# Attention with a step for row maxima: half of the weighted-value groups cut into two column halves, the output copied out by ScalarE alone, the maxima transposed one place later in VectorE's order

## The chip, the core and the metric

The kernel runs on one core of one Trainium2 chip. The metric is device time in microseconds for one execution; the time of a kernel is the median of several executions.

## What is computed

The reference is one transformer block without learned norms: layer norm, softmax attention with 32 heads of 16 columns, a residual, layer norm, a gMLP mixer, a residual. The change concerns the attention alone.

```
x: 1 x 2048 x 512;  H = 32 heads, Dh = 16
q, k, v = split(layernorm(x) @ wqkv)
p = softmax(q k^T * Dh**-0.5)          # 32 heads, 2048 x 2048 scores each
o = p v
h = x + o @ wo
z = gelu(layernorm(h) @ w_in);  z1, z2 = halves of z
out = h + (z1 * (w_sp @ layernorm(z2) + b_sp)) @ w_out
```

## The kernel before

**Stages.** First the projections q, k, v (about 0 to 165 us of the profile); then the attention (about 165 to 1410 us); then the output projection, the gMLP product with the 2048 x 2048 matrix `w_sp`, and the last projection.

**Units of the attention.** The heads are taken four at a time (8 groups `hg`), the queries 512 at a time (4 blocks `qb`), the keys 128 at a time (16 blocks `kb`). That makes 512 units. The loop takes two units in each turn, a *pair*: `kb` even, then `kb1` odd. Every 8 pairs one block of 512 queries is finished.

**Scores.** `score(hg, qb, kb, p)` (L673, L676) makes one tile `s` of 128 keys by 2 heads by 512 queries: two matmuls with 50 rows each, one on the rows from 0 and one on the rows from 64 of the array (`t` = 0 and 1), so that these two can run side by side. ScalarE then takes the exponential of the whole tile (1024 columns) into `pt`. A unit has two such tiles, a pair four. Below they are called S0 and S1 (first unit), S' and S'' (second unit). The pool `ps_s` has two places for `s`, which the four tiles use in turn: S0 and S' the one, S1 and S'' the other. So S' waits for the exponential of S0, and S'' for that of S1.

**Weighted values.** `weigh` (L684) adds one unit to the block's output `pv`: four matmuls, one for each head, each 32 columns of the array wide and 512 queries long, side by side. They are float32; the trace shows each as two matmuls, eight in a group. The groups run one unit late: in a pair, the group of the previous pair's second unit comes first (`prev`), and that of the pair's own first unit at the end. One column of the weights is of ones, so that `pv` also carries the softmax sums. `pv` has one PSUM bank.

**Maxima.** The exponent needs each query's largest score. `max_pair(m)` computes it ahead for 128 queries and two heads, in eight steps, each a matmul with 48 rows into one of three PSUM banks (`ps_m`, banks 0 to 2; L225): four steps on the rows from 64 (`four[0]` to `four[3]`, t = 1), two on the rows from 0 (`two` and the step for keys 1536 to 2047, t = 0), each followed by a maximum over 512 columns on VectorE (L230); and `minus` and `plus` (t = 0) for the other keys: ScalarE takes the absolute value of the differences (`minus`, L235), and VectorE adds that to the sums and reduces (`plus`, L239). The pairs of the loop make the maxima 11 pairs ahead: 245 pairs of the 256 hold these eight steps, the last 11 hold none. After every eighth `max_pair` VectorE reduces the parts (L245, `nm`), GpSimd splits them, and `max_rows` (L259, L263) transposes them on VectorE and issues eight DMAs on SyncE's queue that put them into two extra rows of `qst`.

**End of a query block.** At `kb` = 0, `gather` copies `pv` of the finished block to `o`: columns 0 to 255 by VectorE (L690), the others by ScalarE (L694), one after the other. Then eight DMAs store `o` and the sums. At `kb` = 6 `invert` (L648) takes the reciprocal of the sums on VectorE.

**Order.** Inside the attention the order of each engine's instructions is the order in which the code issues them (a manual schedule for TensorE, ScalarE, VectorE and SyncE). A pair before the change, in TensorE's order, where a step's number after "bank" is its PSUM bank:

```
S0, S1, four[0] (bank 2), two (bank 0), group of prev,
minus (bank 1), [gather at kb = 0], four[1] (2), S', four[2] (0), S'',
four[3] (1), plus (2), group of the first unit, [max_rows], last (1)
```

The code that the change touches:

Of the kernel before, what the change touches and what calls it, by code (L numbers as in the profile page):

```python
# [8 lines left out]
F32 = mybir.dt.float32  # L9
# [3 lines left out]
AF = mybir.ActivationFunctionType  # L13
# [5 lines left out]
P = 128  # L19
# [3 lines left out]
DH = 16  # L23
# [3 lines left out]
NB = S // P  # L27
HB = NB // 2
NQ = S // 512
DB = D // P  # L30
HG = H // 4
# [17 lines left out]
def block_kernel(ctx: ExitStack, tc: tile.TileContext, x, wqkv, wo, w_in, w_sp4, b_sp, w_out, out):  # L49
# [154 lines left out]
            return more[i]()  # L204
        return ps_m.tile([P, 512], F32, name=f"m{i}")

    def max_pair(m):

        g, i = divmod(m, 8)
        hg, qb = divmod(g, NQ)
        q, k, w = qst[g], kst[hg % 2], uvs[hg % 2]
        if i == 0:
            mx[g] = sm.tile([P, 16, 4], F32, name="mx")
            nc.gpsimd.memset(mx[g][:, :8, 3:], LOW)
        c, p = slice(i % 4 * P, i % 4 * P + P), i // 4
        at = lambda t, e: mx[g][:, t * 8 + i, e:e + 1]  # L220

        def scores(t, keys, b):
            r = slice(RG * t, RG * t + KS)
            acc = bank(b)
            nc.tensor.matmul(acc, q[r, p, c], keys[r, p], start=True, stop=True)  # L225
            return acc

        def one(t, e, b):
            acc = scores(t, k[:, :, 512 * e:512 * e + 512], b)
            nc.vector.reduce_max(at(t, e if t else e - 1), acc, axis=AX.X)  # L230

        def minus(b):
            acc = scores(0, w[:, :, 512:], b)
            ab[0] = sm.tile([P, 512], F32, name="ab")
            nc.scalar.activation(ab[0], acc, AF.Abs)  # L235

        def plus(b):
            acc = scores(0, w[:, :, :512], b)
            nc.vector.tensor_tensor_reduce(ab[0], acc, ab[0], 0.5, LOW, ALU.add, ALU.max, at(0, 0))  # L239

        def last(b):
            one(0, 3, b)
            if i == 7:
                nm = sm.tile([P, 2, 8], F32, name="nm")
                nc.vector.tensor_reduce(nm.rearrange("p t i -> p (t i)"), mx.pop(g), axis=AX.X,  # L245
                                        op=ALU.max, negate=True)
                parts = sm.tile([P, 2, 2, 8], F32R, name="mparts")
                split(parts[:, :, 0], parts[:, :, 1], nm, "pool", "pool")
                turned[0] = (g, parts)

        ab = {}
        four = [lambda b, e=e: one(1, e, b) for e in range(4)]
        return [four[0], lambda b: one(0, 2, b), minus, four[1], four[2], four[3], plus, last]

    def max_rows():

# [398 lines left out]
    with ExitStack() as at:  # L655
# [6 lines left out]
        ps_s = at.enter_context(tc.tile_pool(name="ps_s", bufs=2, space=PSUM))  # L662
        pv = {}

        def score(hg, qb, kb, p):

            q, k = qst[hg * NQ + qb], kst[hg % 2]
            turn[0] += len(later)
            pool = later[0] if later and turn[0] % 3 == 2 else ps_s
            s = pool.tile([P, 2, 512], F32, name="s")  # L670
            for t in range(2):
                r = slice(RG * t, RG * t + KM)
                nc.tensor.matmul(s[:, t, :], k[r, p, kb * P:(kb + 1) * P], q[r, p, :],  # L673
                                 start=True, stop=True)
            t = pp.tile([P, 2, 512], F32, name="pt")
            nc.scalar.activation(t, s, AF.Exp, scale=DH ** -0.5)  # L676
            return t

        def weigh(hg, qb, kb, pts):
            if kb == 0:  # L680
                pv[0] = ps_v.tile([P, 512], F32, name="pv")
            for j in range(4):
                c = (4 * kb + j) * VW
                nc.tensor.matmul(pv[0][32 * j:32 * j + 32, :], vst[hg % 2][:, c:c + 32],  # L684
                                 pts[j % 2][:, j // 2, :], start=kb == 0, stop=kb == NB - 1)

        def gather(hg, qb, pool=sm):

            o = pp.tile([P, 512], F32, name="o", bufs=1)
            nc.vector.tensor_copy(o[:, :256], pv[0][:, :256])  # L690
            if pool is sm and later:
                nc.vector.tensor_copy(o[:, 256:], pv[0][:, 256:])
            else:
                nc.scalar.activation(o[:, 256:], pv[0][:, 256:], AF.Copy)  # L694
            cols = slice(qb * 512, (qb + 1) * 512)
            sums = pool.tile([P, 16], F32, name="sums")
            for j in range(4):
                h = head(hg, j % 2, j // 2)
                nc.sync.dma_start(o_scr[h * DH:(h + 1) * DH, cols], o[32 * j:32 * j + DH, :])
                nc.sync.dma_start(sums[32 * j:32 * j + 32, :], o[32 * j + DH:32 * j + VW, :])  # L700
            sums_[0] = (hg, cols, sums, pool)
# [18 lines left out]
        def more_h(k):  # L720

            for _ in range(k):
                if not pieces:
                    sb = h_rows[len(hns)]
                    acc = later[0].tile([P, 512], F32, name="h")
                    pieces.extend([sb, acc, h_products(sb, acc)])
                sb, acc, products = pieces
                next(products)
                made[0] += 1
                if made[0] % (3 * DB):  # L730
                    continue
                pieces.clear()
                add_h(sb, acc)
                split_o(h_rows[len(hns) + 1], *("pool", "pool") if hns else [None])
                mv, rs = scale_h(sb)
                hns[sb] = e2.tile([P, D], F32, name="hn", bufs=3)
                nc.vector.tensor_scalar(hns[sb], xrs.pop(sb), mv[:, 0:1], rs,
                                        op0=ALU.subtract, op1=ALU.mult)
# [4 lines left out]
        with tc.manual_schedule(engines={E.PE, E.Activation, E.DVE, E.SP}):  # L743
            for n in range(0, len(units), 2):
                (hg, qb, kb), (_, _, kb1) = units[n:n + 2]
                if hg + 1 < HG and n % 64 < 24 and n % 4 == 0:
                    load_k(hg + 1, [n % 64 // 4])
                if hg + 1 < HG and n % 64 < 12 and n % 4 == 2:
                    load_uv(hg + 1, [n % 64 // 4])
                if hg + 1 < HG and n % 64 == 30:  # L750
                    load_v(hg + 1)
                if kb == 2 and n // NB + 3 < HG * NQ:
                    load_q(n // NB + 3)
                steps = max_pair(m) if m < 8 * HG * NQ else []
                m += 1
                if not steps and not later:
                    maxima.close()
                    later.append(attn.enter_context(
                        tc.tile_pool(name="ps_l", bufs=1, space=PSUM, side="right")))
                step = lambda b: steps and steps.pop(0)(b)  # L760
                pts = [score(hg, qb, kb, 0), score(hg, qb, kb, 1)]
                step(2)
                step(0)
                if prev is None:

                    pv[0] = ps_v.tile([P, 512], F32, name="pv")
                    for j in range(4):
                        nc.tensor.matmul(pv[0][32 * j:32 * j + 32, :], vst[0][:, :32],
                                         vst[0][:, :512], start=True, stop=True)
                else:  # L770
                    weigh(*prev)
                step(1)
                if kb == 0 and n:
                    gather(*units[n - 1][:2])
                step(2)
                pts1 = [score(hg, qb, kb1, 0)]
                step(0)
                pts1.append(score(hg, qb, kb1, 1))
                step(1)
                step(2)  # L780
                if n >= 490:
                    more_h(2 + (n < 494))
                weigh(hg, qb, kb, pts)
                if turned:
                    max_rows()
                step(1)
                prev = (hg, qb, kb1, pts1)
                if kb == 6 and n > NB:
                    invert()
                if n % 32 == 16 and n < 6 * 32:  # L790
                    load_weights(n // 32)
                if n in (476, 482, 492, 504):
                    load_o(h_rows[(476, 482, 492, 504).index(n)])
                if n == 482:
                    split_o(h_rows[0], "pool", "pool")
            weigh(*prev)
            gather(*prev[:2], e2)
# [186 lines left out]
    with ExitStack() as fin:  # L984
# [29 lines left out]
        def product(acc, a, b, blocks=range(HB)):  # L1014
            for k in blocks:
                mm3(acc, a[0][:, k, :], a[1][:, k, :], b[0][:, k, :], b[1][:, k, :],
                    k == 0, k == HB - 1)
# [299 lines left out]
```

## Time and profile before

| | |
|---|---|
| median of 3 runs | 1864.46 us (1864.09 to 1864.78) |
| the profiled execution | 1863.55 us |
| its span, first to last instruction | 1861.7 us |
| TensorE busy / VectorE / ScalarE / GpSimd | 1852.8 / 1530.4 / 1317.8 / 225.7 us |
| exponentials of the attention (L676) | 1024 instructions, 994.1 us |
| maxima on VectorE (L230, L239) | 1508 and 249 records, 956.6 and 169.6 us |
| weighted values on TensorE (L684) | 4096 matmul records, 545.8 us |
| granted TensorE clock | 1.000 |

The busy time of TensorE is modelled from pipelined matmuls, and a few records can be missing, so a busy share near 100% does not say that TensorE works at its peak: a matmul that waits behind another one counts as busy. What the other engines and the order in time say has to be read beside it. Groups of instructions give the busy time, the mean of one and what ended the idle time before them; a chain of waits follows the end of the program back from releaser to releaser.

### The profile page before, as it was taken

How to read it: one execution, taken by the hardware profiler on the slowest of the kernel's cores; microseconds unless marked ns; L12 is line 12 of the kernel's file. 1: busy time of each engine (PE TensorE's matmuls, PEld its weight loads, DVE VectorE, ACT ScalarE, POOL GpSimd, SP SyncE). 2: the span in 40 equal slices, each digit the busy share in tenths (PEclk: the TensorE clock that was granted, in tenths of full speed). 3: DMA queues.
4: the chain of work that ended last, by engine and by line, in shares of the span. 5: the costliest groups of instructions: out<-in, count | busy, mean ns of one | idle time of the engine just before them, and what ended most of it. 6: DMA issues, size and time to landing. Idle time of an engine off the chain costs nothing.

```text
span 1861.7 us, 31964 instructions
## 1 busy us (share of the span) xinstructions
PE 1852.8 (100%) x11410; PEld 1047.3 (56%) x11410; DVE 1530.4 (82%) x3060; ACT 1317.8 (71%) x1696; POOL 225.7 (12%) x305
## 2 busy tenths in 40 slices
PE   9999999999999999999999999999999999999999
PEld 6775444444444444444444444444437889999998
DVE  6487999999999999999999999999935766877664
ACT  3224888888888888888888888888895444434221
POOL 2241000011010100000000000000001756001111
PEclk9999999999999999999999999999999999999999
DMA  6688111221120121022011112100123555768662
GB/s 192 193 191 197 41 24 30 48 53 28 39 57 15 49 44 25 13 51 40 13 39 32 23 29 50 25 14 13 30 56 108 175 160 166 226 186 264 212 191 94
DMA packets 148743, 159.90 MB, mean 86 GB/s; under 512 B 63096, under 2 KB 93320, under 8 KB 147240
## 3 DMA queue, kind: packets, MB, share of 16 engines
q1 hardware_dynamic: 143800, 146.44, 29.7%
q10 hardware_dynamic: 4752, 11.41, 1.6%
q8 instruction: 90, 1.47, 0.3%
q14 instruction: 69, 0.57, 0.1%
q0 software_dynamic: 32, 0.01, 0.0%
HBM read 101.26 MB, written 55.61 MB: 84 GB/s over the span
## 4 chain that ended last, share of the span: by engine, by line
PE 98%; DVE 1%; issue 0%; ACT 0%; DMA 0%; SPq 0%; POOL 0%; POOLq 0%; DVEq 0%; ACTq 0%
PE pv L684 27%; PE m L225 26%; PE s L673 13%; PE acc L96 5%; PE acc L98 5%; PE acc L97 5%; PE g L98 4%; PE g L97 4%; PE g L96 4%; PE acc L617 2%; PE tp L1189 1%; PE h L617 0%; PE tp L885 0%; PE acc L1210 0%; PE tp L369 0%
## 5 line engine op out<-in xcount | busy, mean ns | idle before, releaser
L676 ACT ACTIVATE pt<-s 128x1024 f32<-128x1024 f32 x1024 | 994.1, 1030 | 141.6 <-PE s L673 139.2
L230 DVE TENSOR_REDUCE mx<-m 128x1 f32<-128x512 f32 x1508 | 956.6, 684 | 99.7 <-PE m L225 56.6
L225 PE MATMUL m<-kst,qst 48*128 48x512 f32 x1508 | 605.1, 447 | 0.0
L684 PE MATMUL pv<-pt,vst 128*32 128x512 f32 x4096 | 545.8, 605 | 0.0
L673 PE MATMUL s<-qst,kst 50*128 50x512 f32 x2048 | 465.1, 428 | 0.0
L225 PEld LDWEIGHTS m<-kst,qst 48*128 48x128 f32 x1508 | 262.7, 184 | 316.2 <-DVE mx L230 221.4
L673 PEld LDWEIGHTS s<-qst,kst 50*128 50x128 f32 x2048 | 222.6, 185 | 53.9 <-ACT pt L676 29.8
L225 PE MATMUL m<-uvs,qst 48*128 48x512 f32 x497 | 246.5, 496 | 0.0
L225 PEld LDWEIGHTS m<-uvs,qst 48*128 48x128 f32 x497 | 90.8, 183 | 205.4 <-DVE mx L230 204.6
L684 PEld LDWEIGHTS pv<-pt,vst 128*32 128x32 f32 x4096 | 80.8, 108 | 158.2 <-issue 155.5
L239 DVE CUSTOM_DVE_ANT_0 ab<-m,ab 128x512 f32<-128x512 f32 x249 | 169.6, 681 | 0.0
L235 ACT ACTIVATE ab<-m 128x512 f32<-128x512 f32 x248 | 149.3, 602 | 4.1 <-PE m L225 4.0
L90 POOL CAST mparts<-nm 128x16 fp32r<-128x16 f32 x32 | 6.3, 197 | 880.2 <-DVE nm L245 880.2
L825 ACT ACTIVATE ws<-a 128x512 fp32r<-128x512 f32 x80 | 45.8, 621 | 50.0 <-PE g L98 23.6
L904 ACT ACTIVATE z<-acc 128x464 f32<-128x464 f32 (+2 forms) x64 | 27.6, 456 | 65.3 <-PE acc L98 63.3
L96 PE MATMUL acc<-wi,hT 128*128 128x464 f32 (+2 forms) x196 | 72.8, 371 | 0.0
L98 PE MATMUL acc<-wi,hT 128*128 128x464 f32 (+2 forms) x196 | 71.8, 366 | 0.0
L97 PE MATMUL acc<-wi,hT 128*128 128x464 f32 (+2 forms) x196 | 71.6, 365 | 0.0
L826 DVE TENSOR_TENSOR ws<-a,ws 128x512 fp32r<-128x512 f32 x80 | 56.1, 745 | 13.1 <-ACT ws L825 13.0
L96 PE MATMUL g<-b,ws 128*128 128x344 f32 x192 | 62.6, 326 | 0.0
L88 ACT ACTIVATE part<-acc 128x512 fp32r<-128x512 f32 x32 | 19.1, 598 | 60.8 <-PE acc L98 56.0
L98 PE MATMUL g<-t,ws 128*128 128x344 f32 x192 | 61.3, 319 | 0.0
(200 smaller groups left out, 2121.2 us busy)
## 6 DMA issues: line engine op xcount, KB each, us to landing
a<-in_w_sp SPq DMA_DIRECT2D x80, 256.0 KB
qst<-q_scr SPq DMA_DIRECT2D x192, 64.0 KB
z_scr<-z ACTq DMA_DIRECT2D x32, 344.0 KB
kst<-k_scr SPq DMA_DIRECT2D x42, 256.0 KB
k_scr<-part SPq DMA_DIRECT2D x16, 512.0 KB
q_scr<-part SPq DMA_DIRECT2D x16, 512.0 KB
z<-z_scr SPq DMA_DIRECT2D x14, 344.0 KB
b<-z_scr SPq DMA_DIRECT2D x24, 172.0 KB
```

The costliest lines, as they stand in the source:

```text
L96: nc.tensor.matmul(ps, lh, rh, start=first, stop=False)
L97: nc.tensor.matmul(ps, lh, rl, start=False, stop=False)
L98: nc.tensor.matmul(ps, ll, rh, start=False, stop=last)
L225: nc.tensor.matmul(acc, q[r, p, c], keys[r, p], start=True, stop=True)
L230: nc.vector.reduce_max(at(t, e if t else e - 1), acc, axis=AX.X)
L235: nc.scalar.activation(ab[0], acc, AF.Abs)
L239: nc.vector.tensor_tensor_reduce(ab[0], acc, ab[0], 0.5, LOW, ALU.add, ALU.max, at(0, 0))
L673: nc.tensor.matmul(s[:, t, :], k[r, p, kb * P:(kb + 1) * P], q[r, p, :], start=True, stop=True)
L676: nc.scalar.activation(t, s, AF.Exp, scale=DH ** -0.5)
L684: nc.tensor.matmul(pv[0][32 * j:32 * j + 32, :], vst[hg % 2][:, c:c + 32], pts[j % 2][:, j // 2, :], start=kb == 0, stop=kb == NB - 1)
L825: nc.scalar.activation(hi, src, AF.Copy)
L826: (nc.gpsimd if el == "pool" else nc.vector).tensor_sub(lo, src, hi.bitcast(F32))
```

## The change

Only the 245 pairs with maxima change, and `gather`. The order of the eight steps of `max_pair` in the loop becomes `minus, four[0], two, (keys 1536 on), four[1], four[2], plus, four[3]`; elsewhere it stays. The score tiles S1 and S'' are made in two pieces, each of one matmul, with other work between the two (`scores_of`). The group of `prev` is cut into two halves of 256 columns each, set apart, in every pair but those with `kb` = 0 (214 pairs). `gather` copies all 512 columns of `pv` by ScalarE in 30 of its 32 calls. `max_rows` runs after the first VectorE step of the following pair and no longer at that pair's end. A pair after the change, in TensorE's order:

```
minus (bank 2), S0 (both), four[0] (1), [max_rows], S1 first piece,
half group of prev (at kb = 0 the whole, then gather),
two (0), S1 second piece, keys 1536 on (1), four[1] (2), S' (both),
other half group of prev (not at kb = 0),
S'' first piece, four[2] (0), plus (1), S'' second piece,
group of the first unit, four[3] (0)
```

The matmuls of the weighted values become 1192 of 512 columns and 1712 of 256 columns in the program, where there were 2048 of 512 columns. No other engine gets more or fewer instructions but VectorE and ScalarE for `gather`: 30 copies of 256 columns less on VectorE, and on ScalarE 30 of 512 columns in place of 30 of 256.

```diff
         ab = {}
         four = [lambda b, e=e: one(1, e, b) for e in range(4)]
-        return [four[0], lambda b: one(0, 2, b), minus, four[1], four[2], four[3], plus, last]
+        two = lambda b: one(0, 2, b)
+        if late:
+            return [minus, four[0], two, lambda b: one(0, 3, b), four[1], four[2], plus,
+                    lambda b: last(b, 1, 3)]
+        return [four[0], two, minus, four[1], four[2], four[3], plus, lambda b: last(b, 0, 3)]
...
-        def score(hg, qb, kb, p):
+        def score(*unit):
+            first, second = scores_of(*unit)
+            first()
+            return second()
+
+        def scores_of(hg, qb, kb, p):
...
-            for t in range(2):
+
+            def product(t):
                 r = slice(RG * t, RG * t + KM)
                 nc.tensor.matmul(s[:, t, :], k[r, p, kb * P:(kb + 1) * P], q[r, p, :],
                                  start=True, stop=True)
-            t = pp.tile([P, 2, 512], F32, name="pt")
-            nc.scalar.activation(t, s, AF.Exp, scale=DH ** -0.5)
-            return t
-
-        def weigh(hg, qb, kb, pts):
+            def second():
+                product(1)
+                t = pp.tile([P, 2, 512], F32, name="pt")
+                nc.scalar.activation(t, s, AF.Exp, scale=DH ** -0.5)
+                return t
+
+            return lambda: product(0), second
+
+        def weigh(hg, qb, kb, pts, cols=slice(0, 512)):
...
-                nc.tensor.matmul(pv[0][32 * j:32 * j + 32, :], vst[hg % 2][:, c:c + 32],
-                                 pts[j % 2][:, j // 2, :], start=kb == 0, stop=kb == NB - 1)
+                nc.tensor.matmul(pv[0][32 * j:32 * j + 32, cols], vst[hg % 2][:, c:c + 32],
+                                 pts[j % 2][:, j // 2, cols], start=kb == 0,
+                                 stop=kb == NB - 1 and cols.stop == 512)
 
         def gather(hg, qb, pool=sm):
             o = pp.tile([P, 512], F32, name="o", bufs=1)
-            nc.vector.tensor_copy(o[:, :256], pv[0][:, :256])
-            if pool is sm and later:
-                nc.vector.tensor_copy(o[:, 256:], pv[0][:, 256:])
+            if pool is sm and not later:
+                nc.scalar.activation(o, pv[0], AF.Copy)
             else:
-                nc.scalar.activation(o[:, 256:], pv[0][:, 256:], AF.Copy)
+                nc.vector.tensor_copy(o[:, :256], pv[0][:, :256])
...
-                step = lambda b: steps and steps.pop(0)(b)
-                pts = [score(hg, qb, kb, 0), score(hg, qb, kb, 1)]
-                step(2)
-                step(0)
...
+                if steps:
+                    step = lambda b: steps.pop(0)(b)
+                    step(2)
+                    pts = [score(hg, qb, kb, 0)]
+                    step(1)
+                    if turned:
+                        max_rows()
+                    first, second = scores_of(hg, qb, kb, 1)
+                    first()
...
+                        weigh(*prev, *[slice(0, 256)] * (kb > 0))
+                        if kb == 0:
+                            gather(*prev[:2])
+                    step(0)
+                    pts.append(second())
+                    step(1)
+                    step(2)
+                    pts1 = [score(hg, qb, kb1, 0)]
+                    if kb:
+                        weigh(*prev, slice(256, 512))
+                    first, second = scores_of(hg, qb, kb1, 1)
+                    first()
+                    step(0)
+                    step(1)
+                    pts1.append(second())
+                    weigh(hg, qb, kb, pts)
+                    step(0)
```

More of the change, by code (lines that the diff above doesn't have):

```diff
@@ L205, in bank, with max_pair @@
         return ps_m.tile([P, 512], F32, name=f"m{i}")
-    def max_pair(m):
+    def max_pair(m, late=False):
         g, i = divmod(m, 8)
@@ L239, in plus, with last @@
             nc.vector.tensor_tensor_reduce(ab[0], acc, ab[0], 0.5, LOW, ALU.add, ALU.max, at(0, 0))
-        def last(b):
-            one(0, 3, b)
+        def last(b, *which):
+            one(*which, b)
             if i == 7:
@@ L683, in weigh @@
                 c = (4 * kb + j) * VW
-                nc.tensor.matmul(pv[0][32 * j:32 * j + 32, :], vst[hg % 2][:, c:c + 32],
-                                 pts[j % 2][:, j // 2, :], start=kb == 0, stop=kb == NB - 1)
+                nc.tensor.matmul(pv[0][32 * j:32 * j + 32, cols], vst[hg % 2][:, c:c + 32],
+                                 pts[j % 2][:, j // 2, cols], start=kb == 0,
+                                 stop=kb == NB - 1 and cols.stop == 512)
         def gather(hg, qb, pool=sm):
             o = pp.tile([P, 512], F32, name="o", bufs=1)
-            nc.vector.tensor_copy(o[:, :256], pv[0][:, :256])
-            if pool is sm and later:
-                nc.vector.tensor_copy(o[:, 256:], pv[0][:, 256:])
-            else:
-                nc.scalar.activation(o[:, 256:], pv[0][:, 256:], AF.Copy)
+            if pool is sm and not later:
+                nc.scalar.activation(o, pv[0], AF.Copy)
+            else:
+                nc.vector.tensor_copy(o[:, :256], pv[0][:, :256])
+                if later and pool is sm:
+                    nc.vector.tensor_copy(o[:, 256:], pv[0][:, 256:])
+                else:
+                    nc.scalar.activation(o[:, 256:], pv[0][:, 256:], AF.Copy)
             cols = slice(qb * 512, (qb + 1) * 512)
@@ L753, in block_kernel @@
                     load_q(n // NB + 3)
-                steps = max_pair(m) if m < 8 * HG * NQ else []
+                steps = max_pair(m, True) if m < 8 * HG * NQ else []
                 m += 1
@@ L759, in block_kernel @@
                         tc.tile_pool(name="ps_l", bufs=1, space=PSUM, side="right")))
-                step = lambda b: steps and steps.pop(0)(b)
-                pts = [score(hg, qb, kb, 0), score(hg, qb, kb, 1)]
-                step(2)
-                step(0)
[L764 to L769, printed above, removed]
+                if steps:
[7 more added lines that the diff above has]
+                    first()
+                    if prev is None:
+                        pv[0] = ps_v.tile([P, 512], F32, name="pv")
+                        for j in range(4):
+                            nc.tensor.matmul(pv[0][32 * j:32 * j + 32, :], vst[0][:, :32],
+                                             vst[0][:, :512], start=True, stop=True)
+                    else:
+                        weigh(*prev, *[slice(0, 256)] * (kb > 0))
[15 more added lines that the diff above has]
+                    step(0)
@@ L770, in block_kernel @@
                 else:
+                    pts = [score(hg, qb, kb, 0), score(hg, qb, kb, 1)]
                     weigh(*prev)
[L772 to L786, printed above, removed]
+                    if kb == 0:
+                        gather(*units[n - 1][:2])
+                    pts1 = [score(hg, qb, kb1, 0), score(hg, qb, kb1, 1)]
+                    if n >= 490:
+                        more_h(2 + (n < 494))
+                    weigh(hg, qb, kb, pts)
+                    if turned:
+                        max_rows()
                 prev = (hg, qb, kb1, pts1)
```

## The prediction

> **What bounds the kernel now.** I read the page first, its busy times, its chain and its costliest groups.
>
> ```profile
> span 1861.7 us, 31964 instructions
> ...
> PE 98%; DVE 1%; issue 0%; ACT 0%; DMA 0%; SPq 0%; POOL 0%; POOLq 0%; DVEq 0%; ACTq 0%
> PE pv L684 27%; PE m L225 26%; PE s L673 13%; PE acc L96 5%; PE acc L98 5%; PE acc L97 5%; PE g L98 4%; PE g L97 4%; PE g L96 4%; PE acc L617 2%; PE tp L1189 1%; PE h L617 0%; PE tp L885 0%; PE acc L1210 0%; PE tp L369 0%
> ```
>
> The chain lies on TensorE, two thirds of it in the three lines of the attention (27 + 26 + 13%). A TensorE entry here can hide a wait, so I next took the busy times of eight pairs (one query block), between the same step of one pair and of the eighth after it.
>
> ```profile
> 711.16:750.14 38.98, 38.98 (x260) 16.05 (x257) 35.88 (x69) 34.47 (x42) 1.51 (x4) 1.00 0.18 29
> ```
>
> The columns after the window are its length and the busy time of PE, PEld, DVE, ACT and POOL. Eight pairs take 38.98 us. VectorE (35.88) and ScalarE (34.47) each have about half a microsecond to spare per pair. So no one engine alone sets the pair: the order on TensorE and its waits for the other two do. The clock is 1.00. To see the order I read the chain over one pair, with start, length, what.
>
> ```profile
> 706.39 0.43 PE m L225 x2
> 706.82 0.23 PE s L673 x2
> 707.06 0.23 PE m L225
> 707.29 0.23 PE s L673
> 707.52 0.61 PE m L225 x2
> 708.13 0.99 PE pv L684 x8
> 709.12 0.43 PE m L225
> 709.55 0.46 PE s L673 x4
> 710.00 0.23 PE m L225 x2
> 710.23 0.99 PE pv L684 x8
> 711.23 0.43 PE m L225 x2
> ```
>
> Two matmuls on the two row halves run side by side in 0.23 us; I call that a *wave*. The first wave behind a group of weighted values takes 0.43. A group takes 0.99. Between the groups lie four waves (709.12 to 710.23) and five (706.39 to 708.13). The five would take 0.43 + 4 x 0.23 = 1.35 and take 1.74: there are the waits. TensorE's own work in a pair is 2 x 0.99 + 2 x 0.43 + 7 x 0.23 = 4.45 us, the pair is 711.23 - 706.39 = 4.84, and 0.39 is waiting. For whom, the rows of the other engines in that pair tell.
>
> ```profile
> 706.89 1.89 DVE L230 TENSOR_REDUCE mx<-m 128x1 f32<-128x512 f32 x3 [0.28 <-PE m L225]
> 708.69 0.68 DVE L239 CUSTOM_DVE_ANT_0 ab<-m,ab 128x512 f32<-128x512 f32 x1
> ...
> 709.59 1.89 DVE L230 TENSOR_REDUCE mx<-m 128x1 f32<-128x512 f32 x3 [0.20 <-PE s L673]
> 711.73 0.69 DVE L230 TENSOR_REDUCE mx<-m 128x1 f32<-128x512 f32 x1 [0.26 <-PE m L225]
> ```
> ```profile
> 706.85 0.60 ACT L235 ACTIVATE ab<-m 128x512 f32<-128x512 f32 x1
> 707.35 1.94 ACT L676 ACTIVATE pt<-s 128x1024 f32<-128x1024 f32 x2
> 709.88 1.94 ACT L676 ACTIVATE pt<-s 128x1024 f32<-128x1024 f32 x2 [0.59 <-PE s L673]
> 711.71 0.60 ACT L235 ACTIVATE ab<-m 128x512 f32<-128x512 f32 x1
> ```
> ```profile
> L676 ACT ACTIVATE pt<-s 128x1024 f32<-128x1024 f32 x1024 | 994.1, 1030 | 141.6 <-PE s L673 139.2
> ```
>
> Prices from these. A reduction starts 0.06 after its wave ends (706.82, 706.89), lasts 0.69, and the next queued one starts 0.60 later ((1.89 - 0.69)/2). An exponential starts 0.10 after its wave (709.78, 709.88), lasts 1.03, the next starts 0.91 later (1.94 - 1.03); the absolute value starts 0.05 after its wave and the exponential behind it 0.50 later (706.85, 707.35). A matmul that waits for a PSUM bank ends 0.54 after the bank's reader: `plus` waits for the reduction that ran from 706.89 to 707.58, and its wave ends at 708.13.
>
> With these I walk the old pair from the end of a group (0): four waves to 1.12, group to 2.11, `minus` and `four[1]` to 2.54, S' 2.77, `four[2]` 3.00; the exponential of S1 ends at 2.71, so S'' ends at 3.25; `plus` waits for a reduction that ends at 3.29 and ends at 3.83; group to 4.82. The trace has 4.84; the walk is short by 0.02 to 0.05 of pairs of 4.84 to 4.87.
>
> **The change: TensorE's work.** The new order pairs all matmuls: (last, `minus`), S0, (`four[0]`, S1 first), half group, (`two`, S1 second), (keys 1536 on, `four[1]`), S', half group, (S'' first, `four[2]`), (`plus`, S'' second), group. That is eight waves for nine, 0.23 us less, but three groups for two, so one 0.20 more for the slower first wave (0.43 - 0.23), and the second half's own cost.
>
> ```profile
> 705.78 0.61 PE L684 MATMUL pv<-pt,vst 128*32 128x512 f32 x4
> ...
> 708.05 1.07 PE L684 MATMUL pv<-pt,vst 128*32 128x512 f32 x8
> ```
>
> A group is two passes 0.46 apart (1.07 - 0.61). No trace here has a pass of 256 columns. Halving takes away at most one pass's time, so a half costs at least 0.99 - 0.46 = 0.53, and at most the whole 0.99; below 0.53 nothing points. I take 0.56, near the low end, since columns streamed are nearly all of a pass. Work after: 0.99 + 2 x 0.56 + 3 x 0.43 + 5 x 0.23 = 4.55 us, 0.10 more than 4.45. What can be won is only the 0.39 of waits.
>
> On that slower first wave there is a rule. The Trainium skill, page "TensorE: Matmul & The Clock Gate", section "Step-by-step: what each phase is for", says that the drain of one matmul overlaps the fill of the next, so a stream of them costs little beyond its columns; by it the cut would be free. The skill's page "TensorEngine Tiling (Array Packing)", section "Key Properties", says that changing the tiling mode drains TensorE; the 0.43 behind each group agrees with that one.
>
> **Its waits.** The new pair from the end of a group: last and `minus` to 0.43; S0 0.66; `four[0]`, S1 first 0.89; half 1.45; `two`, S1 second 1.88. VectorE begins last's reduction at 0.49 and `four[0]`'s behind it at 1.09; that one ends at 1.78, and the wave of keys 1536 on needs its bank: it ends at 2.32 in place of 2.11, a wait of 0.21. S' 2.55 (the exponential of S0 starts behind the absolute value, 0.48 + 0.50 = 0.98, ends 2.01, and allows 2.55: just in time). Half 3.11. S'' first 3.54; S1's exponential runs from 1.98 to 3.01 and allows 3.55: in time again. `plus`, S'' second 3.78; group to 4.77. With the shortfall of the old walk 4.80: a plain pair is 0.06 faster than 4.86, the mean of those in the window (below).
>
> **Three pairs of eight are not plain.** Their extras stand in VectorE's or ScalarE's queue.
>
> ```profile
> 660.85 0.69 DVE L230 TENSOR_REDUCE mx<-m 128x1 f32<-128x512 f32 x1 [0.20 <-PE s L673]
> 661.58 0.22 DVE L245 TENSOR_REDUCE nm<-mx 128x16 f32<-128x64 f32 x1
> 661.71 3.17 DVE L230 TENSOR_REDUCE mx<-m 128x1 f32<-128x512 f32 x5
> ...
> 665.40 0.21 DVE L259 STREAM_TRANSPOSE mturned<-mparts 128x32 f32<-128x32 f32 x1
> ```
> ```profile
> 695.60 0.24 DVE L648 RECIPROCAL rcp<-sums 128x16 f32<-128x16 f32 x1
> 695.76 1.22 DVE L230 TENSOR_REDUCE mx<-m 128x1 f32<-128x512 f32 x2
> ```
> ```profile
> 638.07 0.50 PE L225 MATMUL m<-uvs,qst 48*128 48x512 f32 x1
> ...
> 643.05 0.50 PE L225 MATMUL m<-uvs,qst 48*128 48x512 f32 x1
> ```
> ```profile
> 639.11 0.40 ACT L694 ACTIVATE o<-pv 128x256 f32<-128x256 f32 x1
> ```
>
> - `nm` stands between last's and `four[0]`'s reduction and moves the latter from 0.60 to 0.86 behind (660.85 to 661.71). Before, `four[0]`'s bank was not needed soon; now the wait grows by that 0.26. The transposition, moved behind `four[0]`, holds `two`'s reduction by up to 0.21, hence `plus`'s bank by about 0.05. Pair: 4.80 + 0.31 = 5.11. GpSimd's split and the eight DMAs come about a pair earlier on SyncE's queue, where nothing waits for them.
> - `invert`'s reciprocal in the same place costs 0.16 (695.60 to 695.76): 4.96.
> - At `kb` = 0 the group stays whole, and S1's second matmul stands behind it: group to 1.88, wave 2.31. The copy of `pv`, now 512 columns, starts in ScalarE's queue at about 1.9 behind S0's exponential and holds S1's by 0.50 (as the absolute value of 512 does), to 2.41, which is when S1 is ready anyhow: the longer copy costs nothing, its cover being the whole group; without it, up to 0.50. But S1's exponential ends at 3.44, and with no half group between, S'' waits for it and ends at 3.98; 4.21; group to 5.20, with the shortfall 5.23. Before: 643.05 - 638.07 = 4.98.
>
> VectorE's copies that go (0.41 each, 30 of them) lie in its idle time and win nothing.
>
> Old: 38.98 for eight; less the 4.98, the others average 4.86. New: 5 x 4.80 + 5.11 + 4.96 + 5.23 = 39.30. That is 0.32 more, for 245/8 = 30.6 blocks: 9.8 us. On the profiled execution's 1863.55 (1.85 around the span): 1873.4; the median of the runs is 0.9 above that execution: **1874 us**.
>
> **The rivals.**
> 1. *Faster: the third change of groups is free.* Two halves with their first waves then take no more than one whole group, 0.33 less than in my sum (2 x 0.56 - 0.99 + 0.20), 0.16 in each. The first saving vanishes in the wait for the bank of `four[0]`; the second brings S'' only to 3.45, where S1's exponential (now 1.88 to 2.91) holds it. Seven of eight pairs win 0.10: 0.70 less per eight, 38.60, 30.6 x -0.38 = -11.6 us: 1853. It ends not slower once a half and its first wave cost some 0.05 less than I take. Against it: every group in the chain has its 0.43. If the waits behind `nm` and the reciprocal should also be hidden, about 1840. The drain-overlap rule of the skill's TensorE page above would give this case.
> 2. *Slower by much: a half keeps more than its share.* If it costs 0.66, the first excess hides in the bank's wait, the second does not: 0.10 in seven of eight pairs, 21 us: 1895. At 0.99 it would be 0.65 each, 139 us: 2013. For it: eight more weight loads and matmuls a pair, unseen at this size; against it, the 0.46 per pass.
> 3. *No change:* the plain pairs win 0.12 rather than 0.06 and pay for the three others: 1864.5. S' and S'' arrive within 0.01 of their exponentials, so 0.05 either way is easy.
>
> **How the numbers follow.** A measurement of this kernel tells about 0.2% (3.7 us) from no change. The forecast's case, slower by 4 to 25 us, has 0.48; rival 1 0.28; rival 2 0.15; rival 3 0.09. Faster 0.28, within 0.2% 0.09, slower 0.63. The range goes from rival 1 to past the milder form of rival 2: 1849 to 1900; 0.09 lies below (rival 1's further form), 0.07 above.
>
> **What would show it.** In the changed trace: eight pairs take 39.3 us, plain ones 4.80, the one after `nm` 5.1, those with `gather` 5.2; the wave behind each half takes 0.43 and a half 0.56; the wave of keys 1536 on waits for VectorE. Wrong: halves under 0.5 or over 0.65; plain pairs under 4.7; the pairs after `nm` and the reciprocal as long as the others; ScalarE idle before S1's exponential at `kb` = 0 because of the copy.

## The result, and the profile after

The changed kernel takes 1875.38 us (median of 6 runs, 1875.2 to 1877.1), the kernel before 1864.38 in the same comparison: a ratio of 1.006, interval 1.0047 to 1.0073. It is 11.0 us (0.6%) slower; forecast were 1874 us and slower.

The page after, its busy times and its chain:

```profile
span 1873.6 us, 35561 instructions
...
PE 1836.1 (98%) x13122; PEld 1003.6 (54%) x13122; DVE 1517.4 (81%) x3030; ACT 1370.4 (73%) x1696; POOL 225.5 (12%) x305
...
PE 92%; ACT 3%; DVE 3%; issue 1%; POOL 0%; DVEq 0%; POOLq 0%; ACTq 0%
```

TensorE's share of the chain fell from 98 to 92%; VectorE's rose from 1 to 3% and ScalarE's from 0 to 3%. Line numbers differ from kernel to kernel; the tiles tell what a row is: `m` the products for the maxima, `mx` their reductions, `s` the scores, `pt` the exponentials, `pv` the weighted values, `o` the copy. Eight pairs, one query block (window, its length, then the busy time of TensorE, its weight loads, VectorE, ScalarE, GpSimd; 1.00 is the granted clock):

```profile
582.32:621.68 39.36, 38.44 (x314) 14.62 (x312) 35.45 (x68) 36.25 (x42) 4.95 (x5) 1.00 0.12 33
```

39.36 us against 38.98 to 39.00 before, for 30.6 blocks: 11.0 us, all of the loss. The chain over one plain pair after the change (start, length, what):

```profile
631.09 0.43 PE m L225 x2
631.52 0.23 PE s L686 x2
631.75 0.23 PE m L225
631.98 0.01 PE s L686
631.99 0.57 PE pv L703 x8
632.55 0.85 PE m L225 x3
633.40 0.26 PE s L686 x2
633.66 0.57 PE pv L703 x8
634.23 0.70 PE s L686 x2
634.92 1.00 PE pv L703 x8
635.93 0.43 PE m L225 x2
```

The pair takes 635.93 - 631.09 = 4.84 us, 0.02 less than the mean of 4.86 before. There are eight waves and three groups; a half takes 0.57, the wave behind each group 0.43. The 0.85 at 632.55 is the first wave behind the half and the wave of keys 1536 on, 0.43 and 0.42 where an unhindered wave takes 0.23: the wait for `four[0]`'s reduction. The rows of VectorE and ScalarE in that pair:

```profile
631.55 1.29 DVE L230 TENSOR_REDUCE mx<-m 128x1 f32<-128x512 f32 x2 [0.30 <-PE m L225]
633.02 2.48 DVE L230 TENSOR_REDUCE mx<-m 128x1 f32<-128x512 f32 x4 [0.18 <-PE m L225]
```
```profile
632.08 4.00 ACT L692 ACTIVATE pt<-s 128x1024 f32<-128x1024 f32 x4
```

`four[0]`'s reduction is the second of the first row and ends at 632.84; the wave of keys 1536 on starts 0.06 behind it. That is one wait. A second one stands at S'':

```profile
632.90 0.51 PE L225 MATMUL m<-kst,qst 48*128 48x512 f32 x2
```
```profile
634.19 0.18 PEld L686 LDWEIGHTS s<-qst,kst 50*128 50x128 f32 x1 [0.45 <-ACT pt L692]
```

The weight load of S'' waits for S1's exponential, which runs from 633.12 to 634.14. S'' then starts 0.61 behind the start of the second half (633.59), where the wave behind the first half starts 0.57 behind it (631.91 and 632.48): S1's exponential holds the pair by 0.04. ScalarE's four exponentials leave no gap that the row shows, but they are not back to back either: four in a row would take 3 x 0.91 + 1.03 = 3.76 us by the spacing of before, and they take 4.00, because S1 and S'' each start some 0.1 later, about 0.13 behind the end of their scores. The middle of a pair with the copy, by the chain:

```profile
641.67 1.04 PE pv L703 x8
642.71 0.02 issue
642.73 0.45 ACT o L711
643.18 0.04 issue
643.23 1.03 ACT pt L692
644.26 0.04 issue
644.30 0.72 PE s L686 x2
```

Such a pair takes 5.27 us: group, copy, S1's exponential, then S''. The copy counts as the link here, but S1's scores end at 643.10, and by the 0.13 that its exponential started behind them in the plain pair they allow it only at about 643.2 anyhow. The pair behind `nm`, from last's reduction to last's:

```profile
665.93 0.69 DVE L230 TENSOR_REDUCE mx<-m 128x1 f32<-128x512 f32 x1 [0.32 <-PE m L225]
666.66 0.22 DVE L245 TENSOR_REDUCE nm<-mx 128x16 f32<-128x64 f32 x1
666.80 0.68 DVE L230 TENSOR_REDUCE mx<-m 128x1 f32<-128x512 f32 x1
...
670.95 1.29 DVE L230 TENSOR_REDUCE mx<-m 128x1 f32<-128x512 f32 x2 [0.29 <-PE m L225]
```

It takes 5.02 us. Over all blocks the medians of the eight pairs, from the one with the copy on (`minus` to the next `minus` on ScalarE), are 5.27, 4.83, 4.84, 4.84, 4.88 (behind the reciprocal), 5.02 (behind `nm`), 4.84, 4.83; before the change 4.96, then 4.85 to 4.89.

TensorE's rows of the pair behind `nm`:

```profile
667.53 0.50 PE L225 MATMUL m<-kst,qst 48*128 48x512 f32 x2 [0.16 <-DVE mx L230]
...
668.76 0.50 PE L686 MATMUL s<-qst,kst 50*128 50x512 f32 x1
```

The wave of keys 1536 on starts 0.66 behind the wave ahead of it (666.87), where it is 0.42 in the plain pair (632.48, 632.90). S'' starts 0.57 behind the second half (668.19): here S1's exponential no longer holds it.

### The profile page after: what moved, and what is told of

Same layout as the page of the kernel before. It is cut to its first block, busy times and chain, and to the rows that moved or that the text cites. A ratio compares the mean times of both kernels' runs of the same rounds, so it can differ in the third digit from the quotient of the medians.

```text
span 1873.6 us, 35561 instructions
## 1 busy us (share of the span) xinstructions
PE 1836.1 (98%) x13122; PEld 1003.6 (54%) x13122; DVE 1517.4 (81%) x3030; ACT 1370.4 (73%) x1696; POOL 225.5 (12%) x305
## 4 chain that ended last, share of the span: by engine, by line
PE 92%; ACT 3%; DVE 3%; issue 1%; POOL 0%; DVEq 0%; POOLq 0%; ACTq 0%
PE pv L703 28%; PE m L225 20%; PE s L686 13%; PE acc L96 5%; PE acc L98 5%; PE acc L97 5%; PE g L98 4%; PE g L97 4%; PE g L96 4%; DVE mx L230 2%; PE acc L621 2%; ACT pt L692 2%; ACT o L711 1%; PE tp L1230 1%; PE h L621 0%
## 5 line engine op out<-in xcount | busy, mean ns | idle before, releaser
L692 ACT ACTIVATE pt<-s 128x1024 f32<-128x1024 f32 x1024 | 1016.2, 1022 | 16.3 <-PE s L686 7.7
L686 PE MATMUL s<-qst,kst 50*128 50x512 f32 x2048 | 573.2, 423 | 23.1 <-ACT pt L692 23.1
L703 PE MATMUL pv<-pt,vst 128*32 128x256 f32 (+1 forms) x5808 | 591.3, 479 | 0.0
L225 PE MATMUL m<-kst,qst 48*128 48x512 f32 x1508 | 573.3, 475 | 5.5 <-DVE mx L230 4.9
L225 PEld LDWEIGHTS m<-kst,qst 48*128 48x128 f32 x1508 | 228.0, 184 | 393.1 <-DVE mx L230 362.8
L686 PEld LDWEIGHTS s<-qst,kst 50*128 50x128 f32 x2048 | 276.2, 185 | 161.7 <-ACT pt L692 131.4
L703 PEld LDWEIGHTS pv<-pt,vst 128*32 128x32 f32 x5808 | 114.4, 108 | 233.8 <-issue 233.0
L225 PE MATMUL m<-uvs,qst 48*128 48x512 f32 x497 | 221.2, 445 | 0.0
L866 ACT ACTIVATE ws<-s 128x512 fp32r<-128x512 f32 x32 | 19.4, 631 | 57.7 <-DVE s L886 57.7
```

The costliest lines, as they stand in the source:

```text
L703: nc.tensor.matmul(pv[0][32 * j:32 * j + 32, cols], vst[hg % 2][:, c:c + 32], pts[j % 2][:, j // 2, cols], start=kb == 0, stop=kb == NB - ...
L866: nc.scalar.activation(hi, src, AF.Copy)
```

## The experiments

Each is the changed kernel with one edit, unless said otherwise. My theory throughout is the walk of the prediction: three chains (the bank of `four[0]`, S0's exponential, S1's exponential) end nearly together in a plain pair, and one of eight pairs loses to the copy's place, one to `nm`, one to the reciprocal.

**The copy as before, in the new order.**

```diff
-            if pool is sm and not later:
-                nc.scalar.activation(o, pv[0], AF.Copy)
...
+            nc.vector.tensor_copy(o[:, :256], pv[0][:, :256])
...
+                nc.scalar.activation(o[:, 256:], pv[0][:, 256:], AF.Copy)
```

> The changed kernel (1875.4 us) with the output copied out as before the change: columns 0 to 255 by VectorE, then the others by ScalarE. My theory: in the pair with the copy the pair's length hangs on S1's exponential, which stands behind the copy in ScalarE's queue (copy at 642.73, exponential at 643.23, while its scores allow it at about 643.18). A copy that must first wait for VectorE's 0.41 us moves that exponential back by some 0.27 us, 30 times: the pair goes from 5.27 to about 5.5 and the kernel to 1883 us. Rival: the whole copy on ScalarE (0.60 in place of 0.40) is itself what makes this pair long; then the old copy wins about 0.2 us, 30 times, and the kernel takes about 1869 us.

1881.9 us (1.0094 of before, 1.0079 to 1.0109); the pair with the copy went from 5.27 to 5.51. As my theory had it: in the new order the copy by ScalarE alone *saves* 6.5 us, because VectorE's half would stand ahead of it on the way to S1's exponential. The chain of such a pair runs that way: VectorE's copy from 644.77 to 645.20, ScalarE's from 645.22, the exponential from 645.50.

**The copy by ScalarE alone, in the old order** (this kernel is the one before the change with that part alone).

> The kernel before the change with one part of the change alone: the output copied out by ScalarE in one piece of 512 columns, the order untouched. My theory: there the copy stands ahead of the exponential of S' in ScalarE's queue; 0.60 in place of 0.40 moves that exponential, and those of S'' and the next pair's first tile behind it, back by 0.2 us, of which the 0.4 us of ScalarE's idle time before S0's exponential hides a part: at most 0.2 us, 30 times: 1864 to 1870 us, no gain. Rival: VectorE's freed 0.41 us shortens the pair: 4.96 to 4.86, 1861 us.

1870.3 us (1.003 of before, 1.0018 to 1.0043): the pair went from 4.96 to 5.17, at the upper end of what I expected. The exponential of S' starts 0.48 behind the copy (641.48, 641.96), before the change 0.26 (639.11, 639.37). The same edit costs 6 us in one order and saves 6.5 in the other, by what stands behind the copy in ScalarE's queue.

**The group of `prev` left whole.**

```diff
-                        weigh(*prev, *[slice(0, 256)] * (kb > 0))
+                        weigh(*prev)
...
-                    if kb:
-                        weigh(*prev, slice(256, 512))
```

> The changed kernel with the group of the previous pair left whole in all pairs, in the place of its first half; everything else as in the changed kernel. My theory: TensorE's work falls by 0.33 us a pair (one change of groups less), but S1's second product then stands behind the whole group, and S'' waits for S1's exponential, as in the pair with the copy: plain pairs go from 4.84 to about 5.2, 214 of them, +77 us, about 1952 us. Rival: the third change of groups is what the changed kernel loses; without it the pair falls to about 4.74 and the kernel to about 1854 us.

1959.7 us (1.0511 of before, 1.0496 to 1.0527): every pair takes 5.26. One pair of it, by the chain:

```profile
701.12 1.00 PE pv L703 x8
702.12 0.48 PE m L225
...
702.68 1.03 ACT pt L692
703.71 0.04 issue
703.75 0.49 PE s L686
```

TensorE waits through S1's exponential (702.68 to 703.71) because S1's second product stood behind the whole group. So the third change of groups is not what the new order loses by: the two halves cost some 0.35 us of TensorE's work (2 x 0.57 - 0.99, and 0.20 at one more first wave) and spare it a longer wait. The rival is out. This run also tells what the copy costs: its pairs with the copy have a median of 5.26 and those without it have 5.26 too. In the changed kernel the pair with the copy takes 5.27. So there too the whole group makes the pair long, and the copy adds nothing that shows.

**The own group in two halves, adjacent.**

```diff
-                    weigh(hg, qb, kb, pts)
+                    weigh(hg, qb, kb, pts, slice(0, 256))
+                    weigh(hg, qb, kb, pts, slice(256, 512))
```

> The changed kernel with the pair's own group (the third one) also in two halves of 256 columns, but one right behind the other, with no other matmul between. It measures the price of the smaller passes alone. My theory: passes of 256 columns start 0.24 us apart and those of 512 columns 0.45, so the own group grows by 4 x 0.24 - 2 x 0.45 = 0.05 us, at the end of every pair where nothing hides it: 245 x 0.05 = 12 us, about 1887 us. Rival A: the passes are free and all that two halves cost more than one group (2 x 0.57 - 0.99 = 0.15) comes from changing to and fro: 1875 us. Rival B: all the 0.15 is in the passes: +37 us, about 1912 us.

1877.0 us, 1.6 more than the changed kernel: rival A, not my theory. The two kinds of rows of this kernel:

```profile
631.20 1.07 PE L703 MATMUL pv<-pt,vst 128*32 128x256 f32 x16
633.12 0.64 PE L703 MATMUL pv<-pt,vst 128*32 128x256 f32 x8
```

Four passes of 256 columns, adjacent, take the 1.07 us that two of 512 took. The cut itself is next to free (1.6 us for 245 cuts, under 0.01 us each); what two halves cost more than a group (0.57 + 0.57 against 0.99 or 1.00, and a slower first wave) goes with the change from one kind of matmul to the other. The price here is 0.15 for the second group (2 x 0.57 - 0.99) and 0.20 at the wave behind it. The Trainium skill, page "TensorEngine Tiling (Array Packing)", section "Key Properties", says that changing the tiling mode drains TensorE. The place of the price agrees with it. The Trainium skill, page "TensorE: Matmul & The Clock Gate", section "Step-by-step: what each phase is for", says that the drain of one matmul overlaps the fill of the next. The adjacent halves agree with that (1.07 for 1.07), those set apart do not. The two kinds differ in tile shape and also in number format (a weighted-value product shows as two records, a score product as one), and no run separates the two.

**S1's second product ahead of the whole group, at `kb` = 0.**

```diff
                     first()
+                    if kb == 0 and prev is not None:
+                        pts.append(second())
```

> The changed kernel, where only the pair with the copy of the output (30 of 245) is changed: the second product of S1 is issued ahead of the whole group in place of behind it, so that S1's exponential comes before the copy in ScalarE's queue. My theory: that pair is long because S1's exponential starts late and S'' waits for it; freed of that it falls from 5.27 to about 4.8 us, 30 x -0.47 = -14 us, about 1861 us. Rival: the copy of 512 columns by ScalarE is what makes it long; it then holds the exponential of S' in place of that of S1, and the pair stays above 5.1: 1872 us or more.

1880.3 us (1.0086 of before, 1.0071 to 1.0101): a miss, the pair went up to 5.43. The time lies where the rival put it, but not for the rival's reason, the copy, which is not in the chain:

```profile
643.31 0.24 PE s L686 x2
...
645.01 1.30 DVE mx L230 x2
646.31 0.04 issue
646.35 0.49 PE m L225
```

S1's exponential is out of the way, but `two` and the keys from 1536 on come only behind the group, VectorE has nothing until then, and `plus` waits for both reductions (1.30 us). My walk had left out the banks of `four[2]` and `plus`: the whole group starves VectorE as well as ScalarE. In the changed kernel that chain is nearly 0.2 shorter than S1's (the reduction ends at 644.42 and `plus` starts at 644.64); here S1's second product stands by itself ahead of the group, 0.24 more (643.31), and VectorE's chain becomes the longer one.

**The transposition in its old place.**

```diff
-                    if turned:
-                        max_rows()
                     first, second = scores_of(hg, qb, kb, 1)
...
                     weigh(hg, qb, kb, pts)
+                    if turned:
+                        max_rows()
                     step(0)
```

> The changed kernel with the transposition of the maxima (max_rows) back in its old place, ahead of the pair's last step; only the trace is wanted. My theory: nm, between the reductions of last and of four[0], is what makes the pair after it 5.02 us long in place of 4.84; the transposition holds two's reduction but hardly the end of the pair. So this pair goes to between 4.97 and 5.02. Rival: the transposition makes up half of the 0.18 or more, then 4.93 or less.

1875.4 us in one run, the pair behind `nm` 5.03: where the transposition stands makes no difference there. This part of the change shows no worth either way. (The title's "one place later" counts from `nm`: the transposition starts 0.82 us behind `nm`, at 667.48, and 3.82 behind it before the change, so it comes 3 us earlier.)

**`nm` and the reciprocal behind `four[0]`'s reduction.**

```diff
-                nm = sm.tile([P, 2, 8], F32, name="nm")
...
+                pending.append(lambda: gather_max(g))
...
                     step(1)
+                    while pending:
+                        pending.pop(0)()
                     first, second = scores_of(hg, qb, kb, 1)
...
-                    invert()
+                    pending.append(invert)
```

> The changed kernel with VectorE's small instructions moved behind four[0]'s reduction of the following pair, where VectorE is idle for about 0.2 us: nm (and with it GpSimd's split; the transposition follows at the end of that pair), and the reciprocal of invert. The same work, only later. My theory: they cost because they stand between last's and four[0]'s reduction, on the way to the bank for the keys from 1536 on. Moved, the pairs of 5.02 and 4.88 us fall to 4.84: 30 x 0.22 = 6.7 us, about 1868.7 us. Rival: VectorE has no room for them there either: 1875 us.

1868.6 us (1.0026 of before, 1.0015 to 1.0036), 6.8 less than the changed kernel; both pairs take 4.83 to 4.84:

```profile
664.78 0.21 DVE L261 TENSOR_REDUCE nm<-mx 128x16 f32<-128x64 f32 x1
665.05 2.48 DVE L230 TENSOR_REDUCE mx<-m 128x1 f32<-128x512 f32 x4
```

`nm` now lies in VectorE's idle time ahead of `two`. The same instructions, one place later, cost nothing. (The transposition moves to the pair's end in this kernel as well, which the run before shows to be worth nothing.)

**Fewer columns for the first two chains; then for the third; then for a fourth.** These three kernels leave out part of the work, to see which chain holds. The first:

```diff
+            if late and (t, e) == (1, 3):
+                acc = acc[:, :256]
             nc.vector.reduce_max(at(t, e if t else e - 1), acc, axis=AX.X)
...
+            if late:
+                acc = acc[:, :256]
             nc.scalar.activation(ab[0], acc, AF.Abs)
```

> The changed kernel, where in the loop last's reduction and the absolute value with plus take 256 of their 512 columns (so the maxima are of fewer keys). That frees the bank that the wave of keys 1536 on waits for some 0.2 us sooner, and S0's exponential some 0.2 us sooner. My theory: three chains end together in the plain pair, and the third, S1's second product, its exponential, S'', is untouched: the pair goes from 4.84 to 4.80 at best, only the pair after nm wins, 1865 to 1875 us. Rival: the wait for VectorE's reduction is the one that sets the pair: 4.64, 214 x -0.2 = -43 us, about 1832 us.

The second adds

```diff
+                    nc.scalar.activation(t[:, 0], s[:, 0], AF.Exp, scale=DH ** -0.5)
```

for S1 and S''.

> As the kernel before it in this list, and the exponentials of S1 and S'' take one of their two heads (512 of 1024 columns; the weighted values of the other head use the first one's). That shortens the third chain by 0.43 us. My theory: now TensorE's own work is left, 0.99 + 2 x 0.57 + 3 x 0.43 + 5 x 0.23 = 4.57, the plain pair falls to about 4.60, the pair with the copy by some 0.4: about 1806 us. Rival: TensorE is bound at about 4.8 by the order itself: 1860 us or more.

The third cuts the reduction of the keys from 1536 on for t = 0 as well (`if late and e == 3`).

> The kernel with the short exponentials of S1 and S'' (1852 us, plain pair 4.77, where I had said 4.60), with the reduction of the keys from 1536 on (t = 0) also over 256 of its 512 columns. My theory now: there a fourth chain holds, the reduction of two, that of the keys from 1536 on behind it, and then plus, which needs its bank (trace: plus starts 0.04 behind that reduction's end). Cut by 0.27, the pair falls to TensorE's own 4.57 to 4.64: 245 x -0.15 = -37 us, about 1815 us. Rival: the order itself holds TensorE at 4.77; 1850 us.

They took 1868.1, 1852.1 and 1820.6 us (1.0024, 0.9938 and 0.9766 of before). One block of each, in this order, each from its own kernel:

```profile
648.28:687.40 39.12, 37.68 (x314) 14.62 (x312) 31.87 (x68) 34.58 (x42) 0.46 (x3) 1.00 0.26 54
```
```profile
786.54:825.15 38.61, 38.22 (x314) 14.81 (x312) 31.88 (x68) 27.95 (x42) 0.46 (x3) 1.00 0.25 56
```
```profile
808.28:845.87 37.59, 37.28 (x314) 14.25 (x312) 30.03 (x68) 27.90 (x42) 1.51 (x4) 1.00 0.19 37
```

The first: VectorE and ScalarE get shorter and the plain pair stays at 4.84; only the pairs behind `nm` and the reciprocal fall to it. So the wait for VectorE that the chain shows (0.85 at 632.55) is not what sets the pair by itself: remove it, and S1's exponential holds S'', as the chain of a plain pair of that kernel shows:

```profile
654.64 1.03 ACT pt L699
...
655.72 0.49 PE s L693
```

The second: the plain pair falls to 4.77, not to the 4.60 that I had said, and the pair with the copy by 0.06 to 5.20, not by some 0.4. Its rows show a fourth chain:

```profile
701.27 2.48 DVE L232 TENSOR_REDUCE mx<-m 128x1 f32<-128x512 f32 x4 [0.31 <-PE m L225]
...
702.61 0.18 PEld L225 LDWEIGHTS m<-uvs,qst 48*128 48x128 f32 x1 [0.17 <-DVE mx L232]
```

`plus` waits for the second reduction of that row, of the keys from 1536 on, which itself stands behind `two`'s. With that cut the pair is 4.65, near TensorE's own 4.57, at 1820.6 us where I had expected about 1815. So S1's chain comes to 4.84, that of the bank of `four[0]` to about 4.80 (an estimate: the plain pair less the 0.04 by which S1's holds it) and the fourth to 4.77; what S0's would come to by itself no run shows.

**The order of before, at the copy only.** With `nm` and the reciprocal moved as above, the 30 pairs at `kb` = 0 use the old order and the old copy:

```diff
+                turn_pair = kb == 0 and n > 0
+                steps = max_pair(m, not turn_pair, True) if m < 8 * HG * NQ else []
...
+                if steps and turn_pair:
+                    step = lambda b: steps.pop(0)(role[b])
+                    pts = [score(hg, qb, kb, 0), score(hg, qb, kb, 1)]
...
+                    role[0], role[1] = role[1], role[0]
```

> The changed kernel with VectorE's small instructions moved behind four[0]'s reduction, as in the run on them, and in the 30 pairs with the copy of the output the order of before the change (whole groups, copy by VectorE and ScalarE); there the three banks change places, so that each first step finds a bank that is free. My theory: the order of before bears the copy with 0.1 us (4.96 against 4.86), that of the change with 0.43 (5.27 against 4.84). With both, seven pairs take 4.84 and one 4.97: 38.85 for eight against 39.36 of the changed kernel and 39.00 of before, so about 1860 us, 0.2 to 0.25% faster than before the change. Rival: going from one order to the other and back costs as much as is won; 1866 us or more.

1864.7 us (1.0004 of before, 0.9995 to 1.0012): no difference from before, where I had expected 1860. The pair with the copy fell to 4.94 as expected, but the one behind it takes 5.07:

```profile
636.70 0.42 PE m L225
...
641.64 0.43 PE m L225
...
642.07 0.38 PE m L225 x2
642.44 0.32 PE s L694 x2
...
646.71 0.43 PE m L225
```

The two pieces at 642.07 are 0.24 longer than in a plain pair, and that is one wave more. The matmuls ahead of the half start at 641.57, 641.91, 642.14 and 642.37, the half at 642.70; in a plain pair they start at 631.02, 631.36 and 631.59, the half at 631.91. The last step of the old order is on the rows from 0, as `minus`, a product of S0 and S1's first product are: four on these rows and two on the others, where the changed order has three and three. No version that does the whole work is faster than before.

## Why the prediction was right, step by step

- *TensorE's work.* A half was taken as 0.56 and is 0.57; the wave behind it 0.43 and is 0.42 to 0.43. That a half keeps more than half of a group came out right, but not for a reason within the pass: adjacent passes scale with their columns to within 0.01 a group, and the fixed part belongs to the change of groups. That 0.56 lay so near is partly luck, since the forecast's own bounds were 0.53 and 0.99.
- *The plain pair.* Forecast 4.80, measured 4.84: the walk came out 0.04 short. The wait for `four[0]`'s bank is there in its size (the two waves 0.85, forecast 0.44 + 0.43). A wait that the walk had at nothing is there too: it called S'' in time for S1's exponential (1.98 to 3.01 behind the pair's start), which runs from 2.03 to 3.05 (633.12 and 634.14 less 631.09) and holds S'' by 0.04. With 0.02 more in the two halves, the walk's 4.77 comes to 4.83 of the 4.84; the 0.03 that it added for its shortfall covered only a part. So S1's chain, not the bank's, sets the plain pair, by a little; the first shortened kernel bears that out.
- *Behind `nm`*: forecast 5.11, measured 5.02. `four[0]`'s reduction is moved by 0.27 (665.93 to 666.80 for 0.60), about the 0.26 forecast; the pair is longer by 0.18 only. The rows show where the rest goes: the wave of keys 1536 on starts 0.24 later than in a plain pair, and 0.04 of that comes back at S'', which S1's exponential no longer holds; the last 0.02 lie between S' and the second half. The 0.05 for the transposition is nothing.
- *Behind the reciprocal*: forecast 4.96, measured 4.88. The wave of keys 1536 on starts 0.10 later than in a plain pair (661.98 and 662.50, 0.52 for 0.42), not the 0.16 forecast, and the 0.04 at S'' comes back here too.
- *With the copy*: forecast 5.23, measured 5.27. That the whole group covers the longer copy is shown by the kernel with whole groups, whose pairs take 5.26 with the copy and without it; a copy without that cover was measured at 0.2 in the old order.
- *The sum*: 39.30 against 39.36. Plain pairs 5 x 0.04 and the copy 0.04 too low, `nm` and reciprocal 0.09 and 0.08 too high: the errors partly cancel, so the 1.4 us between 1874 and 1875.4 flatters the walk.
- *Rival 1* (the third change of groups free) falls: halves set apart cost 0.35 us more than a group and adjacent ones next to nothing, and the whole group shows what happens without the halves. *Rival 2* falls with a half of 0.57. *Rival 3* would have needed plain pairs of 4.74; none came.

## What to carry to other kernels

When three engines are each near 90% busy, read the pair of instructions that is late and then the one behind it: here three chains come out between 4.77 and 4.84 us, and taking away the wait that the chain of waits shows left the plain pair where it was until the next ones went too. A small instruction costs its place in the queue rather than its length: `nm` and the reciprocal were 6.8 us between two reductions and nothing one place later, and the same copy cost 6 us in one order and saved 6.5 in the other. Cutting a group of matmuls was next to free here; setting the parts apart costs what the change to the other kind of matmul costs, so look at what it buys for the engines that wait.

## What the hardware showed unexpectedly

Four adjacent passes of 256 columns took the 1.07 us of two of 512, so a cut alone has a price under 0.01 us at this size. The change to the column-wise matmuls and back, once more per pair, cost 0.15 us at the groups and 0.20 at the wave behind.
